# New lists of steps and of loads, made with a model in which VectorE and GpSimd share a port, for a fused attention and mixture kernel

## Chip, cores and metric

One Trainium2 chip, one core of it. The metric is device microseconds of one execution; three runs of the kernel before gave 647.9, 650.26 and 651.55 us, so the median is 650.26 us.

## The reference

Three layers follow each other, all in float32. First an attention with random features over 4 batches, 8 heads, 576 positions and 64 dimensions (2304 tokens in all); then a dense layer whose hidden values are multiplied by their own softmax and normalised; then a layer of 8 experts, of which each token takes one.

```python
def phi(x):                       # q and k, scaled by 64 ** -0.25
    proj = einsum('bhsd,md->bhsm', x, omega)              # 128 features
    h = proj - sum(x * x, -1, keepdims=True) / 2
    return exp(h - max(h, -1, keepdims=True)) / sqrt(m)
kv = einsum('bhsm,bhsd->bhmd', k_p, v); z = sum(k_p, axis=2)
attn = einsum('bhsm,bhmd->bhsd', q_p, kv) / (einsum('bhsm,bhm->bhs', q_p, z) + 1e-06)

h = attn_rows @ w_in                                      # 2304 x 512 x 1024
solu = h * softmax(h)
x = ((solu - mean) / sqrt(var + 1e-06) * g_ln) @ w_out    # 2304 x 1024 x 512

e = argmax(x @ w_gate)                                    # one of 8 experts
out = softmax(x @ w_gate)[e] * sigmoid(x @ w_output_gate)[e] * (relu(x @ w1[e]) @ w2[e])
```

## The kernel before

The 2304 tokens are 18 tiles of 128 rows. Everything up to the first expert is written as some sixty kinds of small steps, each a Python function; a step's name is two or three letters and the number of its tile, weight chunk, batch or set. The string `ORDER` (L76 to L118) names all of them once, and the builder runs them in that order. The helper `in_order` ties every instruction to the one before it on its engine, so that each of the five queues (TensorE, VectorE, ScalarE, GpSimd, SyncE) keeps the order of the list. Across engines only data and buffers order the work: GpSimd may run far ahead of where its step stands in the list. `LOADS` (L70 to L75) is the order in which input tiles are fetched on SyncE's queue; the helper `pump` issues the next load as soon as its ring of buffers has room. The experts behind that (from L999 on) are ordinary code and don't depend on the lists.

The steps that matter here:

- `kp`, `kx`, `ke` and `qp`, `qx`, `qe`: projection of a key or query tile on TensorE, its 8 maxima on VectorE (two reductions, L373, from PSUM), its 8 exponentials on ScalarE.
- `kv`, `kw`: sums over keys on TensorE.
- `qz` (GpSimd, L478): exponentials times the key sums, 1024 columns. `qr` (VectorE, L483 to L485): their sum, then the reciprocal. `qs` (GpSimd, L489): exponentials times the reciprocal.
- `qta`, `qtb`, `qca`, `qcb`, `nx`, `xh`, `xl`: transposes of the numerators, the attention product, and its split in a rounded half and a rest.
- `da`, `db`, `dc`, `dd`, `de`, `df`, `dp`, `dg`, `dh`, `dl`: sixteen chunks of `w_in` (0 to 7) and `w_out` (8 to 15) arrive as 64-bit words and are put together into float32 by one ScalarE step (`da`), five VectorE steps in SBUF (L270, L275, L281, L286, L291) and one or two GpSimd steps (`dp` L296 adds the rounding bit that `df` made; `dg` L306 scales `w_out`). `dh` and `dl` split the result into two halves (`dl` is VectorE's L149 with `w1l` or `w2l` as output).
- `ha`, `hb`, `hxa`, `hxb`, `he`, `ma`, `mz`, `mb`, `mc`, `md`, `me`: the dense layer's hidden values and their normalisation.
- `ta`, `tb`, `ca`, `cb`, `sa`, `sb`, `u`, `l`, `ua`, `ub`, `la`, `lo`: transposes, split, second matrix product (`u` and `l`, 24 matmuls each, named `x` in the trace) and store.
- `ra` to `rh`, `za`, `zb`: routing. `zl` and `zm` fetch the first expert's two weights, `wa` and `wb` split the first, `zg` gathers two blocks of its tokens, `zt` transposes them. The expert's first matmuls (`hp<-xteh`) follow `zt`.

The code that this text speaks of, in the words of the two steps between which the port matters:

```python
def df(i):                                          # VectorE
    lo = words[i][:, :, 0]
    nc.vector.tensor_scalar(out=lo, in0=lo, scalar1=28, scalar2=1, op0=ALU.logical_shift_right, op1=ALU.bitwise_and)

def dp(i):                                          # GpSimd, waits for df
    lo, m = words.pop(i)[:, :, 0], singles[i].bitcast(I32)
    nc.gpsimd.tensor_tensor(out=m, in0=m, in1=lo, op=ALU.add)
```

Of the kernel before, what the change touches and what calls it, by code (L numbers as in the profile page):

```python
# [74 lines left out]
ORDER = """  # L75
    da9 wu9 wu5 kp2 kx2 ke2 db9 wu3 kp10 kx10 ke10 dc9 wu5 kp0 kx0 wu3 kp3 da2 ke0 dd9 kx3 ke3 de9 da10 df9 dp9 wu6  # L76
    kp1 db2 kv0 dg9 kp6 kx1 dc2 ke1 ga1 db10 dc10 gb1 kx6 ke6 kv1 dd10 de10 kp4 dd2 kv2 kx4 da1 kp8 kv3 de2 dh9 dl9
    kx8 ke4 df10 dp10 kp7 da11 db11 dc11 dd11 ke8 kv4 dg10 vc0 kx7 ke7 kp5 kx5 ke5 kw4 ga2 df2 db1 dc1 dd1 de1 df1 vz0
    gb2 dp2 dh2 vy0 dh10 dp1 qp0 de11 df11 dp11 dl2 qx0 da8 db8 dc8 kv5 kp9 dg11 kx9 qe0 kv6 dh1 qp1 dl1 ke9 kv7 da7
    vt0 vd0 kv8 qx1 qe1 kp11 vc1 kp14 qz0 qr0 qs0 kv9 db7 dc7 dd7 kx11 de7 ke11 qz1 qta0 dl10 qca0 kx14 ke14 gc2 gd2  # L80
    kp13 dd8 kx13 qtb0 kv10 qcb0 df7 de8 df8 dp8 kp12 kx12 ke13 ga3 gb3 dh11 dg8 qr1 dl11 nx0 ke12 qp2 da0 qs1 da3
    kv11 qp5 qx2 qe2 db0 qx5 qe5 kv12 kv13 dp7 db3 dc3 qz2 dc0 dd0 ga0 dh8 dd3 gc3 vt1 vd1 de3 df3 gb0 de0 dl8 vz1 gd3
    xh0 qta1 qtb1 vy1 qr2 dh7 da4 dl7 dp3 kp15 kx15 vc2 dh3 gc0 xl0 gd0 db4 dc4 qca1 qcb1 kw13 dl3 kp17 kx17 ke15 da5
    ke17 dd4 nx1 qz5 kp16 kx16 ke16 kv14 kv15 df0 qs2 de4 da6 db5 xh1 dp0 dh0 qta2 qca2 qr5 qp4 qs5 df4 dp4 qx4 qe4
    db6 dc5 dd5 dc6 qtb2 kv16 kv17 qta5 dd6 de6 df6 dp6 qcb2 xl1 dl0 qca5 qtb5 qcb5 dh4 qp6 vt2 vd2 qx6 dl4 nx5 dh6
    qe6 qp3 qx3 qe3 de5 df5 qz4 nx2 dl6 qr4 dp5 ha0 xh2 dh5 dl5 qz3 xl2 da13 db13 vz2 dc13 da15 hb0 db15 dd13 de13
    df13 dp13 vy2 hxa0 hxb0 ha1 qr3 he0 dg13 qs4 ma0 da14 hxa1 hb1 hxb1 he1 db14 dc14 ma1 gc1 gd1 ha2 hxa2 vc3 dd14
    de14 mz1 xh5 qs3 vt3 vd3 ga5 gb5 qta3 qtb3 hb2 qca3 qcb3 qta4 qca4 qtb4 qcb4 dc15 dd15 nx3 qz6 xl5 hxb2 he2 df14
    de15 df15 qp7 ma2 qx7 gc5 gd5 mb1 ta1 mc1 ha5 ca1 dp14 qe7 mz2 mb2 mz0 mb0 sa1 dg14 qr6 dp15 dg15 mc0 da12 hb5 tb1
    cb1 hxa5 hxb5 he5 ta0 sb1 ma5 md0 xh3 xl3 nx4 ca0 sa0 ga6 gb6 qp8 qx8 dh15 xh4 ga7 qz7 qr7 ha3 db12 dc12 dd12 de12  # L90
    dh14 gb7 tb0 qs7 qe8 hb3 cb0 sb0 mc2 md2 qta7 xl4 qca7 qs6 qtb7 qcb7 gc7 nx7 hxa3 hxb3 dl15 df12 dp12 he3 gd7 qta6
    qtb6 md1 ma3 qca6 dh13 me0 ta2 ca2 tb2 me2 qcb6 sa2 cb2 mz3 xh7 xl7 qz8 sb2 gc6 gd6 dg12 dh12 qr8 qp9 qx9 ha4 hxa4
    nx6 xh6 xl6 mb3 dl12 qe9 mc3 hb4 hxb4 mz5 dl13 he4 ta3 ca3 ga4 gb4 me1 dl14 l1 ma4 sa3 gc4 gd4 mz4 qp12 qx12 qs8
    qta8 mb4 qe12 qz12 zc0 u1 ua1 la1 ta4 ca4 sa4 qtb8 tb4 qr12 qca8 u0 ua0 ub0 ub1 cb4 sb4 mc4 qcb8 md3 qp11 qx11 lo1
    qe11 l0 la0 qz9 me3 qr9 mb5 qp10 nx8 mc5 xh8 qx10 qe10 ta5 qs9 qz11 qr11 xl8 ha7 hxa7 qs12 qz10 u2 hb7 hxb7 ua2
    ca5 tb3 cb3 sa5 he7 sb3 l2 la2 lo2 ma7 qs11 qta11 qtb11 qta9 qca11 md5 qcb11 qtb9 mz7 mb7 tb5 ub2 ha8 qca9 qcb9
    cb5 hxa8 sb5 hb8 hxb8 he8 mc7 qr10 ma8 md7 qs10 lo0 ta7 ca7 nx11 sa7 u3 ub3 ra0 qp16 qx16 ua3 qta12 rc0 qca12 xh11
    nx9 ha6 xh9 xl9 hb6 xl11 qe16 qtb12 l3 hxa6 hxb6 mz8 he6 ma6 mz6 qp14 qx14 mb8 mb6 rb0 me7 qcb12 nx12 ta6 ca6 sa6
    xh12 la3 rd0 rf0 md4 me4 re0 qe14 ha9 hxa9 xl12 vz3 vy3 qz14 lo3 tb7 me5 rg1 tb6 u5 ub5 cb7 sb7 mc6 md6 cb6 sb6
    hb9 qta10 hxb9 qca10 he9 ma9 rg0 u4 ub4 ua4 qp17 qr14 mc8 mz9 rh0 mb9 qtb10 qcb10 qx17 mc9 l5 ua5 la5 lo5 qe17 md9  # L100
    ta9 ca9 rh1 rg2 ha11 hxa11 l4 tb9 nx10 rg3 rh2 rh3 cb9 sa9 la4 lo4 qs14 qta14 qca14 qz16 qtb14 qcb14 sb9 xh10 xl10
    qr16 hb11 hxb11 he11 qs16 qz17 ma11 mz11 ta8 ha10 hb10 ca8 sa8 qr17 hxa10 hxb10 tb8 nx14 xh14 me9 qta16 qca16 xl14
    l9 he10 ma10 mz10 mb10 qtb16 u9 ub9 ua9 la9 mb11 qp13 lo9 qx13 qe13 u6 cb8 ta11 qcb16 ca11 sa11 mc11 u7 ua7 qs17
    ub7 sb8 me6 ub6 ua6 ha14 hxa14 nx16 ra1 rc1 qz13 qr13 qta17 qs13 qtb17 qca17 qcb17 xh16 hb14 hxb14 he14 qp15 qx15
    qe15 l6 la6 ha12 l7 tb11 ma14 hxa12 qta13 qtb13 qz15 xl16 qca13 qcb13 la7 lo7 rb1 md8 me8 nx13 mz14 qr15 qs15 hb12
    xh13 xl13 hxb12 he12 ma12 mz12 rd1 ha13 hxa13 hb13 hxb13 mb14 mc14 cb11 mc10 he13 ma13 md11 md10 mb12 ta14 nx17
    xh17 xl17 sb11 u8 ua8 ub8 qta15 qca15 mz13 mb13 l8 la8 qtb15 qcb15 ta12 tb12 lo8 lo6 rf1 ta10 u11 re1 rg5 ca10
    nx15 mc12 sa10 me11 ub11 rg4 ua11 xh15 me10 tb10 cb10 sb10 xl15 u10 ub10 ra2 rc2 rd2 ca12 rh4 ca14 sa12 l10 ua10
    la10 lo10 md14 rb2 sa14 re2 cb12 ha16 hb16 mc13 md12 tb14 za0 zl0 cb14 sb12 me14 hxa16 hxb16 he16 ma16 ha15 hxa15
    me12 u12 ub12 ua12 hb15 hxb15 he15 ha17 rg6 ma15 wa0 rh5 l12 la12 hb17 ta13 ca13 mz15 hxa17 md13 sb14 mz16 rh6  # L110
    hxb17 he17 ma17 u14 l11 la11 tb13 cb13 lo11 mb15 mc15 mb16 ta16 rg7 tb16 rf2 rg8 mz17 rh7 sa13 sb13 ca16 u13 sa16
    ua14 ub14 ta15 ca15 l14 rg9 mb17 mc17 rh8 rh9 la14 me13 ub13 ra3 rc3 ta17 tb17 lo12 sa15 rd3 ca17 l13 cb16 rg11
    rb3 rg10 rh10 md15 me15 wb0 cb17 sb17 ua13 rf3 rh11 tb15 cb15 sb16 sb15 u15 ub15 md17 me17 la13 lo13 re3 wa1 wb1
# [1065 lines left out]
```

## Time and profile before

| | us |
|---|---|
| median of three runs (lowest, highest) | 650.26 (647.9, 651.55) |
| the profiled execution | 651.54 |
| its span, first to last instruction | 649.9 |

The profiled execution is 1.3 us above the median. Its span has three parts. Up to 173 us the weights are put together, keys and queries are projected, and the dense layer begins; from 173 us (the first product with `w_out`) to 408.7 us TensorE works through the dense layer; from there to the end it works on the experts. A page gives busy time by engine; what an engine waits for is read from the list of waits, and how long one instruction takes from groups of instructions or, one by one, from the timeline. Matmuls overlap, so TensorE's busy time is more than its work.

### The profile page before, as it was taken

Reading aid. Unit: us, or ns where it says so; the run is one execution under the profiler, and the core shown is the slowest. Engines: PE = TensorE matmul, PEld = TensorE weight load, DVE = VectorE, ACT = ScalarE, POOL = GpSimd, SP = SyncE. Lnnn points to the kernel's source line nnn. Section 1 sums busy time; section 2 is a strip of 40 time slices with the busy share of each in tenths; the row PEclk is TensorE's granted clock in tenths of the full one; section 3 lists DMA queues with packets and bytes.
Section 4 is the critical chain, followed back from the end, with each engine's and each line's share of the span. In section 5 each row is a group of like instructions: output and inputs, shape, how many; then the busy total and the mean of one; then the engine's idle time right before and its main releaser. Section 6 shows DMA issues by size and latency. Waiting matters only on the chain.

```text
span 649.9 us, 12591 instructions
## 1 busy us (share of the span) xinstructions
...
## 2 busy tenths in 40 slices
...
GB/s 292 277 262 181 137 68 1 49 99 17 17 50 33 2 17 18 17 17 18 17 34 130 32 18 205 23 81 310 202 77 123 178 104 130 17 49 10 2 48 27
DMA packets 35075, 55.03 MB, mean 85 GB/s; under 512 B 2559, under 2 KB 21375, under 8 KB 35008
## 3 DMA queue, kind: packets, MB, share of 16 engines
...
## 4 chain that ended last, share of the span: by engine, by line
PE 65%; DVE 18%; issue 8%; DMA 4%; POOL 3%; ACT 2%; POOLq 0%; SPq 0%; DVEq 0%; ACTq 0%
PE x L161 15%; PE hp L161 14%; PE h L161 12%; PE yp L161 12%; PE qT L165 2%; DVE w1l L149 2%; PE lT L165 2%; PE xT L161 2%; DMA out_y<-y,idxs 2%; DVE f L275 2%; DMA wout<-in_w_out 2%; PE qps L161 2%; DVE f L281 1%; DVE qmx L373 1%; DVE kmx L373 1%
## 5 line engine op out<-in xcount | busy, mean ns | idle before, releaser
L161 PE MATMUL x<-w2h,ltl 128*128 128x272 f32 (+1 forms) x288 | 83.2, 289 | 2.8 <-DVE ltl L149 2.8
L161 PE MATMUL x<-w2h,lth 128*128 128x272 f32 (+1 forms) x288 | 84.8, 294 | 0.0
L161 PE MATMUL x<-w2l,lth 128*128 128x272 f32 (+1 forms) x288 | 82.8, 288 | 0.0
L957 DVE SCALAR_TENSOR_TENSOR htl<-hp,hth 128x304 fp32r<-128x304 f32 (+2 forms) x64 | 30.4, 475 | 84.8 <-ACT hth L956 72.4
L161 PE MATMUL hp<-xth,w1h 128*128 128x304 f32 (+1 forms) x224 | 68.6, 306 | 0.7 <-DVE htl L957 0.7
L161 PE MATMUL hp<-xtl,w1h 128*128 128x304 f32 (+1 forms) x224 | 68.4, 305 | 0.0
L161 PE MATMUL hp<-xth,w1l 128*128 128x304 f32 (+1 forms) x224 | 68.0, 304 | 0.0
L161 PE MATMUL yp<-w2h,hth 128*128 128x512 f32 (+1 forms) x160 | 64.1, 401 | 0.0
L161 PE MATMUL yp<-w2h,htl 128*128 128x512 f32 (+1 forms) x160 | 63.5, 397 | 0.0
L161 PE MATMUL yp<-w2l,hth 128*128 128x512 f32 (+1 forms) x160 | 63.4, 396 | 0.0
L161 PE MATMUL h<-w1h,xth 128*128 128x512 f32 x144 | 59.4, 413 | 1.9 <-ACT qe L380 1.9
L956 ACT ACTIVATE hth<-hp 128x304 fp32r<-128x304 f32 (+2 forms) x64 | 27.2, 424 | 71.1 <-PE hp L161 69.6
L161 PE MATMUL h<-w1l,xth 128*128 128x512 f32 x144 | 57.3, 398 | 2.2 <-DVE w1l L149 2.2
L161 PEld LDWEIGHTS x<-w2h,ltl 128*128 128x128 f32 x288 | 55.4, 192 | 3.1 <-DVE ltl L149 3.1
L161 PE MATMUL h<-w1h,xtl 128*128 128x512 f32 x144 | 57.1, 397 | 0.0
L161 PEld LDWEIGHTS x<-w2h,lth 128*128 128x128 f32 x288 | 55.1, 191 | 0.9 <-issue 0.3
L161 PEld LDWEIGHTS x<-w2l,lth 128*128 128x128 f32 x288 | 55.3, 192 | 0.3
L577 POOL TENSOR_SCALAR s<-s,st 128x1024 f32<-128x1024 f32 x18 | 21.6, 1201 | 90.0 <-DVE st L573 66.8
L478 POOL TENSOR_TENSOR pz<-qe,zb 128x1024 f32<-128x1024 f32 (+1 forms) x20 | 49.3, 2464 | 12.4 <-ACT qe L380 7.2
L149 DVE TENSOR_TENSOR xtl<-xT,xth 128x512 fp32r<-128x512 f32 (+1 forms) x36 | 24.1, 671 | 50.5 <-ACT xth L862 44.9
L980 POOL DMA_INDIRECT out_y<-y,idxs x20 | 20.1, 1004 | 77.2 <-ACT y L979 70.3
L489 POOL TENSOR_TENSOR qe<-qe,rd 128x1024 f32<-128x1024 f32 x18 | 35.0, 1951 | 35.7 <-DVE rd L485 35.7
...
## 6 DMA issues: line engine op xcount, KB each, us to landing
raw<-in_w POOLq DMA_DIRECT2D x12, 1024.0 KB
...
raw<-in_w SPq DMA_DIRECT2D x4, 1024.0 KB, 6.0
```

Source lines behind the costliest of these rows:

```text
L149: return eng.tensor_tensor(out=out_, in0=a, in1=hi.bitcast(F32), op=ALU.subtract)
L161: return in_turn(nc.tensor.matmul(ps, **kw))
L165: return in_turn(nc.tensor.transpose(ps, x, ident[0:k, 0:k]))
L275: nc.vector.tensor_scalar(out=m, in0=m, scalar1=3, scalar2=0x3FFFFFFF, op0=ALU.logical_shift_left, op1=ALU.bitwise_and)
L281: nc.vector.scalar_tensor_tensor(out=m, in0=lo, scalar=29, in1=m, op0=ALU.logical_shift_right, op1=ALU.bitwise_or)
L373: nc.vector.tensor_reduce(out=nmx[:, j, :], in_=of[kind, t][j], axis=AX.X, op=ALU.max, negate=True)
L478: nc.gpsimd.tensor_tensor(out=pz[r0:r1], in0=of["qe", t][r0:r1], in1=of["zb", b][r0:r1], op=ALU.mult)
L489: nc.gpsimd.tensor_tensor(out=e3, in0=e3, in1=of.pop(("rd", t)).to_broadcast([P, H, M]), op=ALU.mult)
L577: nc.gpsimd.tensor_scalar(out=s, in0=s, scalar1=st[:, 10:11], scalar2=st[:, 11:12], op0=ALU.mult, op1=ALU.add)
L956: act = nc.scalar.activation(out=hi, in_=ps[:, 0:n], func=AF.Relu)
L957: dve = nc.vector.scalar_tensor_tensor(out=lo, in0=ps[:, 0:n], scalar=0.0, in1=hi.bitcast(F32), op0=ALU.max, op1=ALU.subtract)
L980: nc.gpsimd.indirect_dma_start(out=out, out_offset=bass.IndirectOffsetOnAxis(ap=idxs[0:k, col:col + 1], axis=0), in_=y, in_offset=None, bo ...
```

## The change

Both strings are replaced; nothing else. Lines behind them stand one lower (L149 becomes L150, and so on), since the new `ORDER` has one line more. The same steps stand in both, each once, except the warm-up matmuls on TensorE (`wu`), 31 before and 36 now. The first and last lines of the lists:

```diff
 LOADS = [(x[0], int(x[1:])) for x in """
-    k2 w9 k10 k0 v0 k3 w2 k1 c0 k7 w10 v1 k6 v2 k4 k8 v3 w1 k5 q1 v4 w11 q0 v6 w3 k17 k12 k14 w0 v5 k9 v8 w8 v7 k15 w7
+    k0 w9 k1 k2 w2 k6 k5 w1 v0 c0 w10 k8 k7 k3 v2 k10 q0 k4 v1 w0 w11 k9 v3 w7 v4 w3 q1 v5 w4 v6 w6 k11 k17 k12 v7 w8
...
-    l15 mc16 ua15 la15 lo15 u16 lo14 rg12 zm0 md16 me16 sa17 rh12 u17 ua16 rg13 rh13 ub16 ra4 rb4 rg14 ub17 rh14 ua17
-    rc4 rd4 zb0 ra5 l16 re4 la16 zg1 zg0 rf4 l17 rg15 la17 lo17 rg16 zt0 zh0 zs0 lo16 zt1 zh1 zs1
+    mc15 md15 cb17 lo13 u16 rg14 me16 ub16 wb0 rh12 sb17 ua16 u15 rg13 me15 ua15 l15 la15 ub15 lo15 ra4 rb4 rc4 rd4
+    rh13 rh14 zb0 zg1 l16 la16 sa17 zg0 u17 ua17 l17 re4 rf4 rg16 ub17 ra5 la17 zm0 zt0 rg15 zh0 zs0 lo17 lo16 zt1 zh1
+    zs1
```

**First place: VectorE, behind the step that lets GpSimd add a rounding bit.** `wout10` is the chunk whose `df` releases `dp10`; `kmx` rows are maxima of key tiles. Before:

```order
L291 TENSOR_SCALAR wout10_130<-wout10_130 128x512
L270 TENSOR_SCALAR f11_510<-f11_510 128x512
L275 TENSOR_SCALAR f11_510<-f11_510 128x512
L281 SCALAR_TENSOR_TENSOR f11_510<-wout11_389,f11_510 128x512
L373 TENSOR_REDUCE kmx7_554<-kps7_0_484 128x4
L373 TENSOR_REDUCE kmx7_554<-kps7_1_485 128x4
```

Now:

```order
L292 TENSOR_SCALAR wout10_130<-wout10_130 128x512
L374 TENSOR_REDUCE kmx3_353<-kps3_0_343 128x4
L374 TENSOR_REDUCE kmx3_353<-kps3_1_344 128x4
L150 TENSOR_TENSOR w1l_72<-f2_178,w1h_71 128x512
L374 TENSOR_REDUCE kmx10_382<-kps10_0_372 128x4
L374 TENSOR_REDUCE kmx10_382<-kps10_1_373 128x4
```

The three steps of chunk 11 that followed at once have moved back; the maxima of a key tile stand in their place.

**Second place: VectorE, behind the reciprocal that lets GpSimd scale query tile 1** (`rd1`; `qs1` follows it on GpSimd). Before:

```order
L483 TENSOR_REDUCE rd1_1042<-pz1_921 128x8
L484 TENSOR_SCALAR rd1_1042<-rd1_1042 128x8
L485 RECIPROCAL rd1_1042<-rd1_1042 128x8
L149 TENSOR_TENSOR w2l_74<-f11_510,w2h_73 128x512
L373 TENSOR_REDUCE qmx2_1122<-qps2_0_1065 128x4
L373 TENSOR_REDUCE qmx2_1122<-qps2_1_1066 128x4
L270 TENSOR_SCALAR f0_1075<-f0_1075 128x512
```

Now:

```order
L484 TENSOR_REDUCE rd1_1016<-pz1_1014 128x8
L485 TENSOR_SCALAR rd1_1016<-rd1_1016 128x8
L486 RECIPROCAL rd1_1016<-rd1_1016 128x8
L374 TENSOR_REDUCE qmx5_1082<-qps5_0_1072 128x4
L374 TENSOR_REDUCE qmx5_1082<-qps5_1_1073 128x4
L339 CAST w2h_73<-wog2_1092 128x16
L150 TENSOR_TENSOR w2l_74<-wog2_1092,w2h_73 128x16
L271 TENSOR_SCALAR f8_996<-f8_996 128x512
```

The subtraction of a weight chunk stood there; now two maxima and two small steps come first.

**Third place: VectorE, ahead of the reduction of query tile 4** (`rd4`). `df4` (chunk `win4`) and the maxima of key tile 16 stand directly ahead of these rows. Now:

```order
L150 TENSOR_TENSOR xtl0_1307<-xT0_1143,xth0_1306 128x512
L484 TENSOR_REDUCE rd5_1506<-pz5_1390 128x8
L485 TENSOR_SCALAR rd5_1506<-rd5_1506 128x8
L486 RECIPROCAL rd5_1506<-rd5_1506 128x8
L374 TENSOR_REDUCE kmx17_1512<-kps17_0_1445 128x4
L374 TENSOR_REDUCE kmx17_1512<-kps17_1_1446 128x4
L150 TENSOR_TENSOR w1l_72<-f4_1291,w1h_71 128x512
L374 TENSOR_REDUCE qmx3_1526<-qps3_0_1515 128x4
L374 TENSOR_REDUCE qmx3_1526<-qps3_1_1516 128x4
L271 TENSOR_SCALAR f5_1538<-f5_1538 128x512
L484 TENSOR_REDUCE rd4_1559<-pz4_1556 128x8
```

and GpSimd's queue over the same stretch, now:

```order
L297 TENSOR_TENSOR f4_1291<-f4_1291,win4_593 128x512
L490 TENSOR_TENSOR qe2_1061<-qe2_1061,rd2_1244 128x1024
L479 TENSOR_TENSOR pz4_1556<-qe4_1318,zb0_811 64x1024
L479 TENSOR_TENSOR pz4_1556<-qe4_1318,zb1_1026 64x1024
L490 TENSOR_TENSOR qe5_1116<-qe5_1116,rd5_1506 128x1024
```

Before, sixteen steps stood between `df4` and `rd4` on VectorE; now it is seven, and GpSimd has four large instructions behind `df4` (the first four of these rows) before `rd4` can start.

## Rows read from the trace of the kernel before

**Rows 1.** Busy time by stretch: us, busy (x instructions) by engine, clock, DMA share, GB/s
```profile
0.00:173.00 173.00, 154.75 (x1980) 130.59 (x1981) 152.00 (x266) 117.87 (x352) 85.75 (x54) 0.94 0.42 131
173.00:408.70 235.70, 229.37 (x1712) 207.70 (x1711) 154.23 (x526) 105.11 (x261) 68.80 (x50) 0.98 0.12 43
```

**Rows 2.** Waits of TensorE: who waited for whom, us in total, times, longest
```profile
PE qT L165 <- ACT ke L380: 3.8, 1, 3.8
PE x L161 <- DVE ltl L149: 2.8, 1, 2.8
...
PE xTe L165 <- DMA xge<-x2d,idxe: 0.8, 1, 0.8
```

**Rows 3.** VectorE's groups by shape, 0 to 173 us: busy us, mean ns, idle before
```profile
L373 DVE TENSOR_REDUCE kmx<-kps 128x4 f32<-128x512 f32 x36 | 23.0, 683 | 9.5 <-PE kps L161 9.3
L275 DVE TENSOR_SCALAR f<-f 128x512 int32<-128x512 int32 x16 | 17.3, 1084 | 0.3
...
L149 DVE TENSOR_TENSOR w1l<-f,w1h 128x512 fp32r<-128x512 f32 x8 | 12.6, 1581 | 0.3 <-ACT w1h L152 0.3
...
L270 DVE TENSOR_SCALAR f<-f 128x512 f32<-128x512 f32 x16 | 9.6, 598 | 1.4 <-ACT f L265 1.4
L281 DVE SCALAR_TENSOR_TENSOR f<-wout,f 128x512 int32<-128x512 int32 x8 | 7.9, 992 | 0.1
...
L281 DVE SCALAR_TENSOR_TENSOR f<-win,f 128x512 int32<-128x512 int32 x8 | 7.5, 951 | 0.2
L286 DVE SCALAR_TENSOR_TENSOR f<-win,f 128x512 int32<-128x512 int32 x8 | 6.5, 812 | 0.1
...
L291 DVE TENSOR_SCALAR wout<-wout 128x512 int32<-128x512 int32 x8 | 5.6, 705 | 0.0
L286 DVE SCALAR_TENSOR_TENSOR f<-wout,f 128x512 int32<-128x512 int32 x8 | 5.5, 690 | 0.1
...
L149 DVE TENSOR_TENSOR w2l<-f,w2h 128x512 fp32r<-128x512 f32 x6 | 5.1, 858 | 0.0
...
L291 DVE TENSOR_SCALAR win<-win 128x512 int32<-128x512 int32 x8 | 3.3, 417 | 0.0
```

**Rows 4.** VectorE's timeline, 66.5 to 84.5 us: start, us, instruction, count
```profile
66.89 0.64 DVE L149 TENSOR_TENSOR w2l<-f,w2h 128x512 fp32r<-128x512 f32 x1
...
70.69 0.41 DVE L270 TENSOR_SCALAR f<-f 128x512 f32<-128x512 f32 x1
71.13 2.97 DVE L275 TENSOR_SCALAR f<-f 128x512 int32<-128x512 int32 x2
...
75.47 0.69 DVE L286 SCALAR_TENSOR_TENSOR f<-win,f 128x512 int32<-128x512 int32 x1
76.08 0.43 DVE L291 TENSOR_SCALAR win<-win 128x512 int32<-128x512 int32 x1
...
79.01 1.21 DVE L483 TENSOR_REDUCE rd<-pz 128x8 f32<-128x1024 f32 x1
...
80.58 2.73 DVE L149 TENSOR_TENSOR w1l<-f,w1h 128x512 fp32r<-128x512 f32 x1
83.24 1.28 DVE L373 TENSOR_REDUCE kmx<-kps 128x4 f32<-128x512 f32 x2
```

**Rows 5.** GpSimd's timeline over the same stretch
```profile
69.25 1.48 POOL L296 TENSOR_TENSOR f<-f,win 128x512 int32<-128x512 int32 x1
71.08 2.40 POOL L478 TENSOR_TENSOR pz<-qe,zb 128x1024 f32<-128x1024 f32 x1 [0.36 <-ACT qe L380]
...
80.36 2.40 POOL L478 TENSOR_TENSOR pz<-qe,zb 128x1024 f32<-128x1024 f32 x1 [2.12 <-ACT zk L447]
82.66 2.41 POOL L489 TENSOR_TENSOR qe<-qe,rd 128x1024 f32<-128x1024 f32 x1
```

**Rows 6.** The chain of waits, 158 to 200 us: the first product with w_out
```profile
172.99 2.86 PE x L161 x24
```

**Rows 7.** DMA issues: line, count, KB each, median us to landing
```profile
raw<-in_w SPq DMA_DIRECT2D x4, 1024.0 KB, 6.0
```

More of the change, by code (lines that the diff above doesn't have):

```diff
@@ L74 @@
+    q14 q11 q13 q16 q15
 """.split()]
 ORDER = """
[L76 to L94, printed above, removed]
@@ L105 @@
[L105 to L109, printed above, removed]
@@ L115 @@
-    rc4 rd4 zb0 ra5 l16 re4 la16 zg1 zg0 rf4 l17 rg15 la17 lo17 rg16 zt0 zh0 zs0 lo16 zt1 zh1 zs1
+    wu9 wu5 kp0 kx0 da9 ke0 db9 dc9 da2 dd9 wu3 kp1 kx1 de9 df9 wu5 kp2 kx2 ke1 db2 dp9 dg9 ke2 dc2 wu6 kp6 dd2 kv0
+    kx6 de2 df2 kp8 da10 db10 da1 ke6 kx8 ga1 gb1 ke8 dc10 dd10 de10 df10 wu3 kp3 kx3 dp2 dh2 dl2 dh9 ke3 wu3 kp10
+    kx10 ke10 db1 kv1 da11 dc1 dl9 dd1 gc1 kp4 kx4 da0 ke4 de1 df1 kv2 db11 kp5 kx5 ke5 db0 dc0 dc11 kv3 kv4 vc0 dd0
+    de0 df0 kp7 kx7 dp10 dg10 dh10 ga2 gb2 dd11 de11 dl10 dp1 dh1 dl1 df11 kw4 ke7 qp0 qx0 da6 db6 kv5 kp11 kx11 da7
@@ new lines @@
+    qe0 dc6 kv6 kv7 db7 dc7 dd7 dp0 ke11 dh0 dd6 de6 df6 dp11 vz0 dg11 de7 vy0 dl0 kp9 kx9 vt0 vd0 wu1 kp14 kx14 da3
+    ke9 qz0 df7 kv8 vc1 qr0 db3 ke14 qp1 qx1 dc3 dp7 dh7 dl7 qe1 kv9 kv10 da8 dd3 de3 qp2 qx2 qs0 qz1 qr1 vz1 vy1 dp6
+    kv11 qta0 qe2 qca0 qp5 qx5 dh6 vt1 gc2 gd2 db8 qs1 vd1 kp12 kx12 qe5 qtb0 qcb0 wu1 qta1 qtb1 dc8 nx0 qca1 qcb1
+    kp13 ke12 ga3 kv12 dd8 de8 df8 gb3 kx13 ke13 qp4 qz2 qr2 dl6 qx4 dp8 dg8 kv13 gd1 df3 kp15 da4 db4 nx1 kx15 xh0
+    dc4 dd4 de4 df4 vc2 qe4 kw13 kp16 kx16 ke15 xl0 xh1 ke16 qz5 kv14 kv15 ga0 kp17 gb0 dp3 dp4 vt2 kv16 dh4 qr5 vd2
```

46 lines of the change are left out of this document (30 added, 16 removed).

## The prediction

> **What bounds the kernel now.** Read the busy times by stretch first [rows 1]. From 173 us to 408.7 us TensorE is busy 229.4 of 235.7 us: little is to be had there. In the first 173 us VectorE is busy 152.0 us and TensorE, as the profile models it, 154.8; ScalarE has 117.9, GpSimd 85.8. TensorE is idle 18.2 us there, and VectorE's 21.0 us of idle time contain 9.3 us of waiting for key projections [rows 3], most of them at the start. So VectorE sets the pace of the first stretch, with TensorE close behind. The list of waits [rows 2] shows single TensorE waits of 2 to 4 us, most of them on VectorE.
>
> Next, what VectorE's time is made of [rows 3]. Its steps of the weight path work in SBUF, and the same operation has very different means: L270 takes 598 ns, L275 1084, L281 951 to 992, the subtraction into `w1l` 1581. The timeline says why. Free, L270 takes 0.41 us, L291 0.43, L286 0.69, the subtraction into `w2l` 0.64 [rows 4]. But at 71.13 us a pair of L275 takes 2.97 us together, while GpSimd runs a `pz` from 71.08 to 73.48; and at 80.58 us the subtraction into `w1l` takes 2.73 us, while GpSimd runs the next `pz` from 80.36 to 82.76 [rows 4, 5]. These VectorE instructions stand still until GpSimd's instruction is over. A reduction does not: at 83.24 us two maxima take 1.28 us, as always, under a running `qe` of 2.41 us [rows 4, 5]. I call the kinds that stand still the shared kinds.
>
> How much is it in all? The ten groups of shared kinds [rows 3] add up to 17.3 + 12.6 + 9.6 + 7.9 + 7.5 + 6.5 + 5.6 + 5.5 + 5.1 + 3.3 = 80.9 us for 94 instructions. Free they would take 48 x 0.42 (L270, L275, L291) + 32 x 0.69 (L281, L286) + 14 x 0.64 (subtractions) = 51.3 us. So 29.6 us of VectorE's 152 us are waits for the port, in the stretch where VectorE sets the pace.
>
> **The change, term by term.** *The same work ahead of the same point.* I count the steps that each list has ahead of the first product with `w_out` (172.99 us now [rows 6]). All 96 shared steps are in both. On VectorE the two sets differ by seven steps against six, on TensorE by a few transposes; by the free prices both are within 1 us. I take nothing for this. The five warm-up matmuls more are at places where TensorE waits for loads; nothing either.
>
> *The port.* GpSimd's additions wait for `df`, its scalings by `rd` for the reciprocal; both then start at once if GpSimd is free. What stands next on VectorE decides whether it is caught. Ahead of the first product there are 16 `df` and 9 reciprocals. Before, a shared kind stands directly behind 10 of the 16 and 6 of the 9; now behind 4 and 4. Elsewhere the maxima of a key or query tile (1.28 us a pair) or other reductions have come between, which run under GpSimd (first and second place in the section on the change). So 16 such places become 8. For the nine products `pz` (one of them in two halves), which wait for ScalarE, the list alone does not tell what they meet. The bounds are plain: none of the 29.6 us saved, or all of it. I take the share that I can count, half: 14.8 us less on VectorE. It lies near the middle because an addition of 1.48 us followed by a scaling, or a product of 2.40 us [rows 5], still outlasts one pair of maxima.
>
> *What of it reaches the end.* Early on, VectorE waits for keys that are still being loaded; time freed there is partly waited away. I give 2 us back for this. And TensorE, busy 154.8 us of the stretch, has waits that the port does not explain, such as 3.8 us for exponentials [rows 2]: 154.8 + 3.8 = 158.6 us is about what the stretch takes once VectorE is out of the way, 14 us below 173. With two engines that near each other each delays the other now and then; another 2.8 us for that. 14.8 - 2 - 2.8 = **10 us** less.
>
> *The end of the list.* Before, TensorE had two products (`l16`, `l17`) between the last row of the routing table and `zt`, and waited 0.8 us for the gathered rows [rows 2]. Now `u17` stands there as well, some 2.9 us more of cover [rows 6], so the 0.8 us go. At worst they stay: `zm` now issues its 2 MB (two transfers of 6.0 us [rows 7]) one store earlier than the gather rather than well ahead, and may slow it. The 2.8 us wait of a product for `ltl` at 368 us [rows 2] comes from splits of the first expert's weight that the builder sets between routing steps; in the new order they stand in the same kind of place, so I leave it.
>
> *Sum.* -10 - 0.8 = -10.8 us. The profiled execution would go from 651.5 to 640.7 us; it was 1.3 us above the median, so against the median of 650.26 us the forecast is **639.5 us**.
>
> **Rivals.** *The port waits only move* (no gain). GpSimd's queue is in order and drifts against the list: a product that starts 2 us later meets other steps. If the new order is caught as often as the old, the 29.6 us stay and only the 0.8 us go: 649.5 us. For it: the list tells only 25 places of 34. Against it: those 25 stand on VectorE's own queue, where the neighbour can't drift away.
>
> *GpSimd is late and VectorE waits for the products* (slower). Nine reductions `rd` stand ahead of the first product with `w_out`. In the third place shown, VectorE has seven steps between `df4` and `rd4`: two pairs of key maxima and one of query maxima (3 x 1.28), one `rd` (1.21 and some 0.4), two subtractions (2 x 0.64) and an L270 (0.42), together 7.2 us; GpSimd has an addition, a scaling and a product in two halves behind `df4`, 1.48 + 2.41 + 2 x 2.40 = 8.7 us [rows 4, 5]. There VectorE waits 1.5 us even if all goes well; before, sixteen steps stood there. If this holds at all nine, 13.5 us are lost and the gain of 10 is more than eaten; the point from which it decides is 1.1 us a product. With one full product of 2.40 us lost at each, 21.6 - 10.8 = 10.8 us slower: 661 us. For it: the new list puts several reductions close behind their products. Against it: GpSimd is busy only 85.8 of 173 us, and where it has slack the product is done early.
>
> The Trainium skill has a rule that speaks for this rival ("SBUF — State Buffer", section "Who interferes with whom"): the port pair is an exclusive lock, whichever engine starts first has it for its whole instruction, and the other blocks fully, so a wait taken from VectorE can come back on GpSimd. The trace agrees on the lock; in its rows VectorE is the loser, and both `pz` keep their 2.40 us [rows 5]. By that rule the 8 waits moved to GpSimd would cost it at most 8 x 0.69 = 5.5 us, and the time would be 645 us if all of it came back through products.
>
> *The first expert's weight is late* (part of the gain lost). Between `zl0` and `wa0`, which splits what it fetches on ScalarE, the list had three products on TensorE and now has one, two of some 2.9 us [rows 6] fewer; the transfers land in 6.0 us each [rows 7]. ScalarE would stand still, VectorE's split behind it, and the wait at 368 us would grow from 2.8 to 5 or 6 us: 642.5 us.
>
> *More than forecast.* TensorE's clock is 0.94 in the first stretch [rows 1], after idle times; fewer of them would bring some of the 0.06 x 173 = 10 us back. With all 18.2 us of its idle time gone, 650.26 - 18.2 - 0.8 = 631 us: the low end.
>
> **How the numbers follow.** Forecast 0.70, of which 0.03 lies below 631; port waits only move 0.14; GpSimd late 0.08; weight late 0.06; more than forecast is 0.02. A measurement of this kernel can tell about 0.5% from no change: faster is below 647.0, slower above 653.5. Faster: 0.70 + 0.06 + 0.02, less 0.04 for small gains, 0.74. Same: 0.14 and those 0.04, less 0.02 that end above: 0.16. Slower: 0.08 + 0.02 = 0.10. The range runs from 631 (all idle time of the stretch gone) to 650.5 (no port wait saved); it leaves out some 0.15.
>
> **What would show it.** In the new profile the ten groups of shared kinds should add up to 63 to 70 us instead of 80.9, with the mean of L275 nearer 0.7 us and that of the `w1l` subtraction nearer 1.1; the first product with `w_out` should start near 162 us; TensorE's idle time before it should be near 10 us, and the wait of `xTe` for the gather gone. The forecast is wrong if the shared kinds still take about 80 us, if L483 shows idle time behind `pz` of over 5 us in the first stretch, or if the first product starts early but the gain is lost before the experts begin.

## The result, and the profile after

The changed kernel takes 624.97 us (median of 4 runs, 623.01 to 625.64) beside 650.85 us for the kernel before on the same chip; the ratio is 0.961 with a 95% interval of 0.957 to 0.964. That is 25.9 us less, and it lies below the range that was given. The profiled execution took 624.91 us, its span 623.1 us. Two executions further on are left out of their kernels' ratios as slow ones: 734.84 us of `new_list_early_zm` (granted clock 0.753) and 630.21 us of `new_list_small_moves`.

Busy time by stretch after the change, cut at the first product with `w_out` (150.9 us; before, the timeline shows it at 172.7) and at the first expert (384.0; before 406.9). The columns are those of [rows 1]: length, then busy time (with the count of instructions) of TensorE, its weight loads, VectorE, ScalarE and GpSimd, then the clock, the DMA share and GB/s.

```profile
0.00:150.90 150.90, 145.57 (x1976) 124.44 (x1976) 133.63 (x267) 117.69 (x351) 82.95 (x54) 1.00 0.48 151
150.90:384.00 233.10, 227.16 (x1724) 205.27 (x1724) 152.82 (x519) 106.13 (x262) 68.52 (x51) 1.00 0.12 44
384.00:623.10 239.10, 229.19 (x1327) 202.78 (x1327) 73.04 (x168) 77.05 (x130) 85.28 (x65) 0.99 0.27 92
```

So 21.8 us of the span's 26.8 come from the first stretch, 1.1 from the second (234.2 before), 3.9 from the experts (243.0). In the first stretch VectorE is busy 18 us less, and the clock column has gone from 0.94 to 1.00.

VectorE's groups in the first stretch, which answer to [rows 3]:

```profile
L374 DVE TENSOR_REDUCE kmx<-kps 128x4 f32<-128x512 f32 x36 | 23.0, 681 | 5.1 <-PE kps L162 4.9
...
L484 DVE TENSOR_REDUCE rd<-pz 128x8 f32<-128x1024 f32 x9 | 10.9, 1209 | 1.1 <-POOL pz L479 1.1
L271 DVE TENSOR_SCALAR f<-f 128x512 f32<-128x512 f32 x16 | 9.8, 610 | 0.0
L150 DVE TENSOR_TENSOR w1l<-f,w1h 128x512 fp32r<-128x512 f32 x8 | 9.3, 1162 | 0.7 <-ACT w1h L153 0.7
L276 DVE TENSOR_SCALAR f<-f 128x512 int32<-128x512 int32 x16 | 8.6, 545 | 0.3
...
L282 DVE SCALAR_TENSOR_TENSOR f<-wout,f 128x512 int32<-128x512 int32 x8 | 5.8, 724 | 0.2
L287 DVE SCALAR_TENSOR_TENSOR f<-wout,f 128x512 int32<-128x512 int32 x8 | 5.5, 689 | 0.2
L287 DVE SCALAR_TENSOR_TENSOR f<-win,f 128x512 int32<-128x512 int32 x8 | 5.5, 687 | 0.1
L150 DVE TENSOR_TENSOR w2l<-f,w2h 128x512 fp32r<-128x512 f32 x6 | 5.5, 911 | 0.0
L282 DVE SCALAR_TENSOR_TENSOR f<-win,f 128x512 int32<-128x512 int32 x8 | 5.4, 688 | 0.1
...
L292 DVE TENSOR_SCALAR win<-win 128x512 int32<-128x512 int32 x8 | 4.1, 517 | 0.0
...
L292 DVE TENSOR_SCALAR wout<-wout 128x512 int32<-128x512 int32 x8 | 3.4, 425 | 0.0
```

The ten groups of shared kinds add up to 62.9 us instead of 80.9. L276 has a mean of 545 ns (L275 before: 1084), the reductions are unchanged (681 ns before 683), and VectorE waits 1.1 us for products `pz`.

TensorE's longest waits, which answer to [rows 2]: the 3.8 and 2.8 us are gone, the wait for the gathered rows is longer.

```profile
PE x L162 <- DVE w2l L150: 2.0, 2, 1.6
PE xTe L166 <- DMA xge<-x2d,idxe: 1.7, 1, 1.7
```

The clock decides how TensorE's busy time is read. A window table of the kernel before, around its longest gap:

```profile
45.00:51.40 6.40, 5.95 (x136) 5.04 (x132) 6.26 (x9) 4.16 (x15) 3.02 (x2) 1.00 0.89 298
51.40:55.20 3.80, 0.04 (x4) 0.00 (x0) 3.80 (x5) 1.18 (x5) 1.43 (x1) 1.00 0.94 270
56.20:63.00 6.80, 6.80 (x75) 5.66 (x76) 4.29 (x10) 5.20 (x18) 1.20 (x1) 0.50 0.25 80
63.00:70.00 7.00, 7.00 (x148) 6.10 (x152) 5.82 (x10) 5.37 (x17) 4.53 (x4) 1.00 0.48 152
```

VectorE's timeline of the same place:

```profile
48.54 2.02 DVE L275 TENSOR_SCALAR f<-f 128x512 int32<-128x512 int32 x1
50.59 2.79 DVE L281 SCALAR_TENSOR_TENSOR f<-win,f 128x512 int32<-128x512 int32 x1
53.30 1.28 DVE L373 TENSOR_REDUCE kmx<-kps 128x4 f32<-128x512 f32 x2
```

TensorE idles while VectorE stands still: two weight steps of 2.02 and 2.79 us lie ahead of the maxima (`kmx`) from which ScalarE makes the exponentials that TensorE needs. Then TensorE runs at half clock (0.50, 1.2 GHz) and does 75 matmuls where the next 7 us have 148. Four such falls lie ahead of the first product, 20.5 us in all; two more follow gaps at 368 and 404 us, 6.8 us each. The changed kernel's profile has none ahead of 618 us (a second profile of it, `after_again`, has two of 3.4 us, at 40.8 and 385.6 us). TensorE's time in the first stretch before is 18.3 us idle, 10.2 us lost at half clock and 144.2 us of work at full clock; after, it is 5.3, 0 and 145.6.

### The profile page after: what moved, and what is told of

Same layout as the page of the kernel before. It is cut to its first block, busy times and chain, and to the rows that moved or that the text cites. A ratio compares the mean times of both kernels' runs of the same rounds, so it can differ in the third digit from the quotient of the medians.

```text
span 623.1 us, 12619 instructions
## 1 busy us (share of the span) xinstructions
PE 601.9 (97%) x5026; PEld 532.5 (85%) x5026; DVE 359.5 (58%) x952; ACT 300.9 (48%) x743; POOL 236.7 (38%) x169
## 4 chain that ended last, share of the span: by engine, by line
PE 71%; DVE 12%; issue 7%; DMA 6%; POOL 1%; ACT 1%; SPq 0%; POOLq 0%; DVEq 0%; ACTq 0%
PE x L162 14%; PE hp L162 14%; PE h L162 14%; PE yp L162 12%; PE qps L162 3%; PE qT L166 3%; PE lT L166 2%; PE kv L162 2%; PE xT L162 2%; DMA out_y<-y,idxs 2%; DVE kmx L374 1%; DVE w2l L150 1%; DMA xge<-x2d,idxe 1%; DMA kr<-in_kT 1%; PE xT L166 1%
## 5 line engine op out<-in xcount | busy, mean ns | idle before, releaser
L162 PE MATMUL x<-w2h,lth 128*128 128x256 f32 (+1 forms) x288 | 83.6, 290 | 0.8 <-DVE w2l L150 0.4
L162 PE MATMUL x<-w2l,lth 128*128 128x256 f32 (+1 forms) x288 | 82.0, 285 | 1.6 <-DVE w2l L150 1.6
L162 PE MATMUL x<-w2h,ltl 128*128 128x256 f32 (+1 forms) x288 | 81.9, 284 | 0.0
L150 DVE TENSOR_TENSOR xtl<-xT,xth 128x512 fp32r<-128x512 f32 (+1 forms) x36 | 24.2, 671 | 50.3 <-ACT xth L863 44.9
L981 POOL DMA_INDIRECT out_y<-y,idxs x20 | 20.1, 1006 | 77.1 <-ACT y L980 75.4
L980 ACT ACTIVATE y<-yp,scs 128x512 f32<-128x512 f32 (+1 forms) x20 | 13.8, 688 | 70.3 <-PE yp L162 62.0
```

Source lines behind the costliest of these rows:

```text
L150: return eng.tensor_tensor(out=out_, in0=a, in1=hi.bitcast(F32), op=ALU.subtract)
L162: return in_turn(nc.tensor.matmul(ps, **kw))
L980: nc.scalar.activation(out=y, in_=ps, func=AF.Copy, scale=scs[0:k, col:col + 1])
L981: nc.gpsimd.indirect_dma_start(out=out, out_offset=bass.IndirectOffsetOnAxis(ap=idxs[0:k, col:col + 1], axis=0), in_=y, in_offset=None, bo ...
```

## The experiments

Three theories stood against each other: the waits for the port (with what follows from them), the clock as a cause of its own, and the order of the loads. The table sets all kernels side by side. "Waiting" is what the 94 shared instructions ahead of the first product take above their free durations (0.42, 0.69, 0.64 us), counted where it is over 0.12 us; "half" is the time at 1.2 GHz; all up to the first product, in us of the profiled execution. In every list the last two of the 96 shared steps start behind the start of the first product (in `new_list_small_moves` ahead of it, so 96 are counted there). With the new list these two wait some 2.2 us more for the port, so that the expectations below speak of 13.6 or 14 us of waits for the changed kernel.

| kernel | waiting | TensorE idle | half | first product | time, ratio to before |
|---|---|---|---|---|---|
| before | 29.9 | 18.3 | 20.5 | 172.7 | |
| changed | 11.5 | 5.3 | 0 | 150.9 | 0.961 [0.957, 0.964] |
| after_again (changed, run again) | 8.8 | 5.0 | 3.4 | 152.0 | 0.961 [0.957, 0.965] |
| fill_gaps | 30.0 | 12.7 | 3.4 | 169.0 | not read |
| four_moves | 25.8 | 16.1 | 20.5 | 168.4 | 0.997 [0.993, 1.000] |
| old_list_reductions_first | 29.1 | 22.4 | 23.9 | 176.7 | 1.005 [1.002, 1.008] |
| before_three_quarters_gpsimd | 16.5 | 10.9 | 0 | 156.5 | not read |
| before_half_gpsimd | 8.2 | 6.0 | 0 | 150.5 | not read |
| before_short_gpsimd | 1.4 | 5.0 | 0 | 148.6 | not read |
| after_short_gpsimd | 0.8 | 3.3 | 0 | 147.7 | not read |
| new_list_more_gpsimd | 24.6 | 14.8 | 10.2 | 164.8 | 0.989 [0.985, 0.994] |
| new_list_old_load_mix | 9.7 | 21.9 | 23.9 | 175.1 | 1.003 [1.000, 1.007] |
| old_list_new_load_mix | 28.8 | 24.1 | 13.7 | 173.3 | 1.004 [1.001, 1.008] |
| tail_fill | 28.8 | 18.7 | 17.1 | 171.6 | 0.995 [0.992, 0.998] |
| new_list_early_zm | 11.1 | 5.1 | 0 | 150.2 | 0.959 [0.953, 0.966] |
| new_list_small_moves | 10.2 | 7.6 | 17.1 | 159.2 | 0.957 [0.953, 0.961] |

"Not read" stands where the kernel leaves work out or spoils later values, so that the time says nothing. `tail_fill` leaves the first stretch as it was and so is a second profile of the old list there: 171.6 us, 1.1 us earlier than the first.

**The port taken away, list unchanged** (`before_short_gpsimd`, `after_short_gpsimd`).

```diff
-            nc.gpsimd.tensor_tensor(out=m, in0=m, in1=lo, op=ALU.add)
+            nc.gpsimd.tensor_tensor(out=m[:, 0:32], in0=m[:, 0:32], in1=lo[:, 0:32], op=ALU.add)
...
-                nc.gpsimd.tensor_tensor(out=pz[r0:r1], in0=of["qe", t][r0:r1], in1=of["zb", b][r0:r1], op=ALU.mult)
+                nc.gpsimd.tensor_tensor(out=pz[r0:r1, 0:1], in0=of["qe", t][r0:r1, 0:1], in1=of["zb", b][r0:r1, 0:1], op=ALU.mult)
...
-            nc.vector.reduce_sum(out=r2, in_=of.pop(("pz", t)), axis=AX.X)
+            of.pop(("pz", t))
+            nc.vector.reduce_sum(out=r2, in_=of["qe", t], axis=AX.X)
```

The scalings of `w_out` and of the queries are cut in the same way.

> The old lists with GpSimd's four large kinds of instruction cut to 32 or 128 columns: rounding bits and scalings of w_out are left out for most columns, the products with the key sums and the scaling of queries for seven heads of eight, and the reciprocal is taken of the plain sum of the exponentials. The values and so the routing are others, so only the stretch up to the first product with w_out is read. Theory P (the gain is the port's and what follows from it): without long GpSimd instructions the old order loses next to nothing, the shared kinds take 52 to 56 us and the first product comes at 148 to 154 us, within 4 us of the new order under the same cut. Theory L (the new order of loads and steps is worth something by itself): it comes at 158 us or later, at least 8 us behind the new order under the same cut.

> The new lists with the same cut of GpSimd's instructions (same parts left out). Only the stretch up to the first product with w_out is read. Theory P: the first product at 146 to 151 us, little better than the new order without the cut (151 us), since few waits for the port are left. Theory L: the same here; the two differ in the old order. If it comes at 143 us or earlier, the 14 us of waits that are left in the new order still cost most of their length.

Measured: the old list comes to its first product at 148.6 us, the new one at 147.7. Between the two lists 0.9 us are left of 21.8. First the old, then the new list:

```profile
0.00:148.60 148.60, 143.58 (x1979) 123.27 (x1979) 124.49 (x264) 116.61 (x352) 24.61 (x54) 1.00 0.49 153
```

```profile
0.00:147.70 147.70, 144.43 (x1977) 123.95 (x1977) 123.51 (x267) 117.06 (x351) 23.97 (x55) 1.00 0.49 154
```

Theory P holds. In the old list the waits cost 24.1 us of time; the 11.5 us that the new list still has cost 3.2. TensorE is now busy 143.6 and 144.4 us of the stretch at full clock, so it is TensorE that sets the end.

**The same cut in steps** (`before_half_gpsimd` with 256 columns and four heads, `before_three_quarters_gpsimd` with 384 and six; same lines).

> The old lists with GpSimd's four large kinds of instruction cut to half their columns: rounding bits and scalings of w_out, products with the key sums and scalings of queries are left out for the other half, and the reciprocal is taken of the plain sum of the exponentials. Only the stretch up to the first product with w_out is read. It halves the port waits without moving a step. Theory F (the waits set the pace until TensorE's own work, about 145 us at full clock, does): some 13 to 16 us of waits are left as in the new order, and the first product comes at 151 to 158 us. Theory G (as in the forecast, TensorE's 159 us are the floor, and half of the waits costs half): 161 to 164 us.

> The old lists with GpSimd's four large kinds of instruction cut to three quarters of their columns (the last quarter of the rounding bits, scalings of w_out, products with the key sums and scalings of queries is left out, and the reciprocal is taken of the plain sum of the exponentials). Only the stretch up to the first product with w_out is read. So far 29.9 us of waits gave 172.7 us, 8.2 gave 150.5, 1.4 gave 148.6. Theory F (one us of wait costs one us down to about 10 us of waits, then TensorE sets the pace and it costs a quarter): 16 to 20 us of waits, and the first product at 157 to 163 us. Theory H (the step from 172.7 to 150.5 comes from a few waits ahead of steps that TensorE needs, which vanish with any shortening): 150 to 154 us.

Measured: 150.5 us with 8.2 us of waits (fewer than expected), 156.5 us with 16.5.

```profile
0.00:156.50 156.50, 145.64 (x1978) 122.75 (x1979) 140.48 (x264) 117.60 (x352) 68.70 (x54) 1.00 0.46 145
```

Without a single step moved, the old list reaches the changed kernel's 150.9 us. From 29.9 to 16.5 us of waits each us is worth 1.2 us (with the half clock that goes too), from 16.5 to 8.2 us 0.7, below that 0.3. Theory F holds, though both times lie half a us below its ranges; Theories G and H fail, and 159 us is no floor. The cut also makes GpSimd's own results earlier. That was not taken apart by a run, but by the lists of waits little hangs on these results in the kernel before: up to the first product VectorE never waits for `pz`, and TensorE waits 0.9 us for GpSimd.

```profile
PE woT L165 <- POOL f L306: 0.9, 1, 0.9
```

ScalarE waits 8.3 us for GpSimd there, but VectorE waits only 0.3 us for what ScalarE then makes for the `w1l` subtractions [rows 3].

**The clock alone** (`fill_gaps`). `wv` is a new step of narrow matmuls without a purpose.

```diff
-    ... de7 ke11 qz1 qta0 ...
+    ... de7 ke11 qz1 wu14 qta0 ...
-    ... dd3 gc3 ...
+    ... dd3 wu5 gc3 ...
-    ... qs6 qtb7 ...
+    ... qs6 wv7 qtb7 ...
```

There are eight `wv` inside `vt3` too, and more ahead of `u13` and around `zt0`. The late ones stand in the bank of the routing table and spoil its sums, so nothing behind the first stretch is read.

> The old lists, in which matmuls without a purpose fill TensorE's longest gaps (3.8 us at 51 us, 1.4 at 78, 2.2 at 125, 2.0 at 155, 2.8 at 368, and the last ones before the first expert); nothing that computes is moved. Theory C (the half speed behind those gaps is a cost of its own): the six stretches at half speed, 34 us in all, go, and with them up to 17 us: the first product with w_out near 163 us instead of 173, the time 634 to 639 us. Theory V (VectorE sets the pace of the first stretch, so TensorE may run slowly there for nothing): TensorE's clock is full but the first product stays within 3 us of 173, and the time is 645 to 650 us.

Measured: 17.1 of the 20.5 us at half clock are gone, which is 8.6 us of work; the first product comes 3.7 us earlier, at 169.0.

```profile
0.00:169.00 169.00, 156.31 (x2045) 132.70 (x2046) 152.42 (x264) 117.71 (x352) 85.75 (x54) 0.99 0.43 135
```

VectorE is as busy as before (152.4 us). Theory V is nearer: in the old list VectorE paces the stretch, and most of what TensorE loses at half clock is hidden. With fewer waits the falls go as well (half and three quarters of the columns, above), but other idle times bring them too (`new_list_old_load_mix`, below). That full clock pays once the waits are gone is argued from this, not run.

**Single moves in the old list** (`four_moves`, `old_list_reductions_first`). The first:

```diff
-    ... qr0 qs0 kv9 db7 dc7 dd7 kx11 ...
+    ... qr0 kx11 qs0 kv9 db7 dc7 dd7 ...
-    ... df3 gb0 de0 dl8 vz1 gd3 ...
+    ... df3 gd3 gb0 de0 dl8 vz1 ...
-    ... he1 db14 dc14 ma1 ...
+    ... he1 ma1 db14 dc14 ...
-    ... dc12 dd12 de12 dh14 gb7 tb0 qs7 qe8 hb3 cb0 sb0 ...
+    ... dc12 dh14 gb7 tb0 qs7 qe8 hb3 cb0 sb0 dd12 de12 ...
```

> The old lists with four moves on VectorE alone, at TensorE's four long gaps of the first stretch: the step that TensorE waits for (the maxima of key tile 11, the small steps of gd3, the reductions ma1, the split sb0) is put ahead of the weight steps that stood still under a GpSimd instruction just before it. Theory A (a wait for the port costs twice where it stands ahead of a step that TensorE waits for: TensorE idles, then its clock halves): the four gaps (9.5 us) shrink and the four falls (10 us of lost work) go; the first product comes 10 to 18 us earlier, the time is 632 to 641 us. Theory V (what counts is the sum of VectorE's time): at most 8 us of waits are moved, half of them saved, so the time is 646 to 648 us.

Measured: 25.8 us of waits are left, 20.5 us at half clock as before; the first product comes 4.3 us earlier, and the time is 646.12 us. Theory A fails, Theory V holds. The second (two of its six moves):

```diff
-    ... df3 gb0 de0 dl8 vz1 gd3 xh0 qta1 qtb1 vy1 qr2 ...
+    ... df3 qr2 gb0 de0 dl8 vz1 gd3 xh0 qta1 qtb1 vy1 ...
-    ... df0 qs2 de4 da6 db5 xh1 dp0 dh0 qta2 qca2 qr5 ...
+    ... df0 qr5 qs2 de4 da6 db5 xh1 dp0 dh0 qta2 qca2 ...
```

> The old lists with six reductions on VectorE moved forward, each to directly behind a step that releases a GpSimd instruction (df11, qr0, df7, df3, df0, df14), so that of the 16 places at which a shared kind stood directly behind a releaser 10 are left. Theory N (the count of such places tells the waits, as in the forecast): 29.9 x 10 / 16 = 19 us of waits, the first product 8 to 13 us earlier. Rival M (the waits only move, since the shared kinds then stand behind the next GpSimd instruction): 24 us of waits or more, the first product at most 6 us earlier.

Measured: 29.1 us of waits, and the first product 4.0 us later, at 176.7. Rival M holds. VectorE's timeline, then GpSimd's, behind the moved `qr2`:

```profile
76.89 1.22 DVE L483 TENSOR_REDUCE rd<-pz 128x8 f32<-128x1024 f32 x1
...
78.60 2.73 DVE L286 SCALAR_TENSOR_TENSOR f<-win,f 128x512 int32<-128x512 int32 x1
81.25 2.38 DVE L149 TENSOR_TENSOR w2l<-f,w2h 128x512 fp32r<-128x512 f32 x1
```

```profile
77.13 1.29 POOL L296 TENSOR_TENSOR f<-f,win 128x512 int32<-128x512 int32 x1 [3.16 <-PE qT L165]
78.37 2.41 POOL L478 TENSOR_TENSOR pz<-qe,zb 128x1024 f32<-128x1024 f32 x1
80.67 2.41 POOL L489 TENSOR_TENSOR qe<-qe,rd 128x1024 f32<-128x1024 f32 x1
```

The reduction passes under the addition as meant; the next two shared instructions then meet `pz` and `qe`, and wait 2.0 and 1.7 us.

**The loads** (`old_list_new_load_mix`, `new_list_old_load_mix`). Only `LOADS` differs; which ring is served next follows the other list, each ring keeps its own order. The new list's first line:

```diff
-    k0 w9 k1 k2 w2 k6 k5 w1 v0 c0 w10 k8 k7 k3 v2 k10 q0 k4 v1 w0 w11 k9 v3 w7 v4 w3 q1 v5 w4 v6 w6 k11 k17 k12 v7 w8
+    k0 w9 k1 k2 v0 k6 w2 k5 c0 k8 w10 v2 k7 v1 k3 k10 v3 w1 q0 k4 v4 w11 k9 v5 w7 q1 k11 w0 k17 v6 k12 v7 w8 w6 v8 k14
```

> The old list of steps; the loads come in the new list's mixture of kinds (which buffer ring is served next), each kind in the old order. Theory P (the port alone): within 3 us of before, either way. Theory L (part of the gain is the loads'): 4 us or more faster.

> The new list of steps; the loads come in the old list's mixture of kinds, each kind in the new order. Theory P: within 3 us of the changed kernel's 625 us. Theory L: 4 us or more slower than that, 629 us or above.

Measured: 652.22 and 652.74 us. The new mixture is worth nothing to the old list, and the old mixture takes the whole gain from the new one, though its waits for the port stay low (9.7 us). Two windows of that kernel, then of the changed one:

```profile
20.00:40.00 20.00, 13.58 (x232) 12.09 (x232) 11.83 (x20) 11.36 (x37) 4.15 (x3) 0.84 0.53 167
40.00:57.00 17.00, 12.83 (x160) 10.42 (x164) 8.23 (x15) 9.36 (x32) 4.09 (x3) 0.50 0.35 116
```

```profile
20.00:40.00 20.00, 18.96 (x418) 16.74 (x417) 19.79 (x37) 19.22 (x65) 7.41 (x6) 1.00 1.01 345
40.00:57.00 17.00, 15.65 (x322) 13.55 (x322) 16.80 (x27) 14.20 (x50) 7.36 (x5) 1.00 0.48 125
```

From 20 to 40 us 167 GB/s come in instead of 345, and VectorE has 11.8 us of work instead of 19.8. With the old list Theory P holds and Theory L fails; with the new list it is the other way round. So the gain belongs to neither string alone: the new list of steps takes the port's waits away, and only with its own loads does that become time.

**More GpSimd in the new list** (`new_list_more_gpsimd`).

```diff
             nc.gpsimd.tensor_tensor(out=e3, in0=e3, in1=of.pop(("rd", t)).to_broadcast([P, H, M]), op=ALU.mult)
+            d = ap.tile([P, H, M], F32, tag="pz", name=f"pd{t}", bufs=1)
+            nc.gpsimd.tensor_tensor(out=d, in0=e3, in1=e3, op=ALU.mult)
```

> The new lists; behind each scaling of a query tile GpSimd squares the tile into a scratch buffer that nothing reads, some 2.4 us more of GpSimd per tile and port to lock (nothing is left out). The waits on VectorE should rise from 13.6 to some 22 to 30 us. Theory F (the sum of the waits decides, in whatever list): the first product at 158 to 168 us instead of 151, and 633 to 643 us in all. Theory S (the new list is shielded: its waits stand where TensorE needs nothing, and GpSimd has slack): 151 to 154 us and under 630 us in all.

Measured: 24.6 us of waits (26.9 counted as in the expectation), first product at 164.8 us, 643.55 us in all, half a us above Theory F's range. Theory S fails, the new list is not shielded: 13.1 us more of waits come with 13.9 us, and two falls to half clock are back. Some of it may be GpSimd's own lateness: TensorE waits 1.6 us for it there, 0.3 us in the changed kernel.

**The end of the list** (`tail_fill`, `new_list_early_zm`, `new_list_small_moves`, `after_again`).

```diff
+                for _ in range(22 if half and t == 13 else 0):
+                    mm(ps[:, 0:cols.stop - cols.start], lhsT=hi[:, 0, :], rhs=w2gh[:, 0, cols], start=True, stop=True)
-    ... rg16 zt0 zh0 zs0 lo16 zt1 zh1 zs1
+    ... rg16 wv3 zt0 zh0 zs0 lo16 zt1 wv10 zh1 zs1
```

> The old lists with TensorE's gaps at 368 us and at 404 to 408 us filled: the first matmul of the product that waits there is done 22 times more, and narrow matmuls without a purpose stand around the transposes of the first expert's tokens. Theory C: the two falls to half speed go (6.8 us each), the first expert comes 2 to 3 us earlier and the experts take 239 us instead of 243; 4 to 6 us less in all. Theory T (those 4 to 5 us come from the new order of the end of the list itself): the falls may go, but the time is less by under 1.5 us.

Measured: 647.74 us, 0.995 [0.992, 0.998], about 3 us less. Both falls are gone and the second stretch is 233.1 us, but in the profiled execution the experts took 242.9: TensorE came to the next gather early, waited 2.5 us for it, and fell to half clock behind it.

```profile
PE xT L165 <- DMA xg<-x2d,idxg: 2.5, 1, 2.5
```

The 3 us lie between the two theories. In the profiled execution the two last stretches are together only 1.2 us shorter than before (233.1 + 242.9 us against 234.2 + 243.0), so how much of the end's gain the two falls explain stays open.

```diff
-    ... ra5 la17 zm0 zt0 ...
+    ... ra5 la17 zt0 ...
-    ... wa1 ca15 ...
+    ... wa1 zm0 ca15 ...
```

> The new lists with one move: zm0, the fetch of the first expert's second weight, stands behind wa1 instead of just ahead of zt0. Theory Z: TensorE's wait for the gathered rows (1.7 and 1.1 us in two executions of the changed kernel) falls below 0.5 us, the stretch from the first product with w_out to the first expert (233 and 232 us) becomes 229 to 231 us, and the time is 621 to 624 us against 625. Rival: the shorter stretch seen with three moves came from the other two; then it stays at 232 to 233 us.

Measured: TensorE's wait for the gathered rows is gone, and the second stretch is 231.4 us instead of 233.1 and 232.2. TensorE's timeline of the changed kernel, then of this one:

```profile
382.20 1.06 PE L166 MATMUL xTe<-ident,xge 128*128 128x128 f32 x8 [1.69 <-DMA xge<-x2d,idxe]
```

```profile
379.54 1.38 PE L166 MATMUL xTe<-ident,xge 128*128 128x128 f32 x8
```

Theory Z holds for the wait; the stretch is 0.4 us above its range. Five runs lie between 620.3 and 627.4 us; the ratio of 0.959 [0.953, 0.966] can't be told from the changed kernel's.

`new_list_small_moves` makes this move and sets `dl14 dl15` directly behind `dl13`.

> The new lists with three small moves: the two last subtractions of w_out weights stand behind that of chunk 13 instead of just ahead of the first product, where one of them waits for the port; and zm0, the fetch of the first expert's second weight, stands behind wa1, some 25 us earlier, so that its 2 MB no longer run beside the gather of the first expert's tokens. Theory Z (zm0 beside the gather makes the gather late): TensorE's wait for the gathered rows, 1.7 us, falls below 0.5 us and its wait of 1.6 us at 153 us goes; 621 to 624 us. Rival (the gather is late because the index comes late): the 1.7 us stay.

> The changed kernel as it is, on the same chip as the others of this group: 622 to 627 us; it gives the scatter against which the three small moves are read.

Measured: 624.01 us, 0.957 [0.953, 0.961], beside 625.22, 0.961 [0.957, 0.965]; the intervals overlap. The wait for the gather is gone here too; that of 1.6 us for the subtractions only moved to just ahead of the first product. Its profile is of the execution of 630.21 us: with 10.2 us of waits the first product came at 159.2 us, after falls of 6.8 and 10.2 us to half clock at 49.7 and 77.1 us. So the sum of the waits alone does not fix the time; why this execution fell is open.

## Why the prediction was wrong

**Right: the work and, by luck, about the port.** Much the same work stands ahead of the first product (1976 matmuls where 1977 were). Of the port's waits some six tenths went, not half: 18.0 us (80.9 to 62.9 us by the ten groups, just below the 63 to 70 named) where 14.8 were forecast. The mean of the `w1l` subtraction is 1.16 us (named 1.1), that of L275, now L276, 0.55 us (named 0.7). That the size came near was luck. The 14.8 us came from a count of shared kinds directly behind a releaser, 16 against 8. With 10 of 16 such places left the old list kept 29.1 of 29.9 us: the count told nothing there, since an instruction that escapes one GpSimd instruction meets the next. (The free price in the prediction adds up to 51.2 us, not 51.3; nothing hangs on it.)

**Wrong: what of it reaches the end.** The step that failed is "154.8 + 3.8 = 158.6 us is about what the stretch takes once VectorE is out of the way". The 154.8 us were taken as TensorE's work, though 20.5 us of them ran at half clock: at full clock they are 144.5. With the waits out of the way (`before_short_gpsimd`) TensorE ends the stretch at 148.6 us, with 143.6 busy. So nothing was to be given back: no run shows the 2 and the 2.8 us that I took off, and 21.8 us came instead of 10, more even than the 18.0 us of waits that went. Down to 156 us each us of waits was worth 1.2 us, with the falls that it brought; only from there on does it shrink, to 0.7 and then 0.3.

The clock stood in the text, as the rival "more than forecast", with 10 us to come back and a chance of 0.02; and the low end of 631 us took the idle time alone. Idle time before a fall and the loss in the fall go together: up to 18.3 + 10.2 us of the stretch were to be had, not 18.2.

The Trainium skill ("Perfetto Trace Analysis", section "Identifying the Most-Contended Engine") says that the matmuls' busy share is no good measure of how close TensorE is to its peak, since matmuls are pipelined, and names the share of peak arithmetic and the busy share of the weight loads instead. The trace agrees that the matmuls' 154.8 us were no measure, but here it was the clock that swelled them. The weight loads were swollen too, and less: 130.6 us [rows 1] in that stretch, 124.0 in the shortest one (`after_short_gpsimd`, 147.7 us).

**Wrong: the end of the list.** The 0.8 us wait was to go; it became 1.7 us. The cause that I had named for the worse case, `zm0`'s 2 MB beside the gather, acted, and by more than its bound (that the 0.8 us stay). The wait at 368 us was left out of the sum, and with it the fall behind it and the one at 408 us. The two later stretches became 5.0 us shorter, not 0.8.

**The rivals.** GpSimd is not late: VectorE waits 1.1 us for products, not 13.5 or 21.6. By the rule of the Trainium skill cited for it ("SBUF — State Buffer", "Who interferes with whom") up to 5.5 us were to come back through GpSimd; the trace does not agree that they did: GpSimd is busy 82.95 us of the first stretch, 85.75 before. The first expert's weight is not late: the wait at 368 us is gone (the rival's count of products between `zl0` and `wa0` was off as well: the lists have four and one, not three and one). And the waits did not merely move, though with the six single moves in the old list they did.

**Open.** At 11.5 us of waits the new list stands at 150.9 us, where the old list's points (8.2 at 150.5, 16.5 at 156.5) give 152.9. Whether these 2.0 us come from the earlier loads, from GpSimd or from scatter was not settled; another execution of the changed kernel had 8.8 us of waits and 152.0, so scatter is as large.
